# The x product of a tile ordered behind the next tile's gate and up gradients, and late gate-gradient tiles transposed by TensorE

## The chip, the cores and the metric

The kernel runs on one core of one Trainium2 chip. The metric is the device time of one execution in microseconds (us). The time before is the median of 8 runs, 528.19 us (527.13 to 531.25). The profile is of one execution, which itself took 527.57 us; its span, from the first to the last instruction of the program, is 525.8 us. The core's engines are called as the profile calls them: PE is TensorE (PEld its weight loads), DVE is VectorE, ACT is ScalarE, POOL is GpSimd and SP is SyncE, which here only issues DMAs.

## The reference

The program computes a forward block and its whole backward pass, for a sequence of 2048 rows of 512 columns in bf16:

```python
xn  = layernorm(x)                                   # x = A_q
s   = xn * (longconv(kv) + kv * ssm_D)               # kv = shiftconv(A_k) * A_v, the long convolution by FFT
z   = (sigmoid(xn @ w_gate) * (xn @ w_up)) @ w_down  # F = 1376
out = x + s * silu(z)
# outputs: out and the gradients of q, k, v, shift_k, ssm_k, ssm_D, w_gate, w_up, w_down for grad_out
```

What matters here is the backward pass of the gated unit. With h = sigmoid(g) * u, it needs for each block of 128 rows

- dz, the gradient of z: grad_out * s times the derivative of silu at z,
- dh = dz @ w_down^T, and from it dg and du, the gradients of the gate and up projections,
- dxn = dg @ w_gate^T + du @ w_up^T (the "x product"), plus what comes through s, and then the backward pass of the layernorm,
- later, over all rows, the three weight gradients.

## The kernel before, in words

**Tiling.** The 2048 rows are 16 tiles of 128 rows (NJ = 16), each [128, 512]; the 1376 columns of the hidden layer are padded to 11 blocks of 128 (NFB = 11), worked in three chunks of 4, 4 and 3 blocks (FBS).

**Stages.** In stage A (to about 155 us of the trace) the FFT convolution forward runs beside the forward products of nine of the tiles (FA, by `f_gen`). Stage B (`stepB`, line 1201, about 155 to 350 us) goes over the tiles i = 0 to 15 and does the remaining seven forward tiles and the backward pass of the gated unit. Stage C (about 350 us to the end) does the backward FFT convolution (`frontC`, `backC`) beside the weight gradients (`dW`), 35 blocks of 16 long matmuls each. `dW` already starts inside stage B, once tile 15's dz exists, and is what PE does alone in the last 16 us.

**The four steps of stage B**, each a Python generator which yields after a piece of work:

- `f_gen(i)` (719): 88 matmuls of 128 columns for gate and up, sigmoid, h; h goes to DRAM for the weight gradients.
- `z_gen(i)` (1114): 11 matmuls of 512 columns for z. Then a chain between ACT and DVE: sigmoid (1127), gate = z * sigmoid (1129), 1 - sigmoid (1131), three DVE steps to `dzA[:, i]` (1132 to 1134). dgate = grad_out * s (1121) enters in the last of these. Then the transpose `dzT`: for tiles 1 to 12 by a DMA transpose that SP issues (1137), for 0, 13, 14 and 15 by four PE transposes into PSUM and a copy (1139 to 1142). After that five more DVE steps (1144 to 1150): out, and `dxa`, the part of dxn that comes through s.
- `d_gen(i)` (1152): three chunks, 44 matmuls of 128 columns in all; each chunk is copied from PSUM by ACT and multiplied twice by DVE into `duT` and `dgT`, which SP also stores to DRAM. For the six tiles whose sigmoid and h were spilled in stage A (15, 13, 11, 9, 7, 5) DVE first forms v from them (two long steps, 1158 and 1159).
- `x_gen(i)` (1180): 22 matmuls of 512 columns into one PSUM bank, which read all of `duT` and `dgT`. Then on DVE dxn (1192, which reads PSUM and `dxa`), a product with a row sum (1193), a small step (1194), on ACT line 1195, on DVE 1196 and 1197; the result is written over the tile of grad_out (`goj`), and POOL stores it from there (1198).

**Order in the program.** Within turn i of the loop at 1209 the steps are: first part of d(i), a part of f(i+4), z(i+1), the loads of tile i+2 (`b_ld`, 1084, two DMAs on POOL), the rest of d(i) mixed with f(i+4), a reload of a spilled tile where there is one, the rest of f, and x(i).

**What the engines then do is set by a planner in the program.** All operations are recorded (`Rec.add`, 240) with a number n in program order and with what they depend on: overlapping SBUF bytes, DRAM blocks, PSUM tiles. `Rec.order` (348) then goes through a modelled time. Each engine takes the operation that can start earliest; of those ready when the engine comes free, the one with the smallest n. It looks ahead by 700 operations (LOOK), about four turns of the loop. It gives out the PSUM banks too: two each for long accumulations (psZ, psX and psW, kind "acc"), two for transposes ("tr"), four for single-bank products. So program order is a priority, and a step that isn't ready is passed over. The engines run their queues in the planned order, whatever comes late.

**Buffers** of stage B are rings (`Ring`, 93): a new use waits for the last reader of the slot. Those of interest: `dxa_r` 2 slots, `dxn_r` 2, `u1_r` 1, `dg_r` and `du_r` 2 each (1073 to 1080), the five tiles of the z chain (`zw`, 1060) one each, and `go_r`, the tiles of grad_out, 4 (1067, 1068). So grad_out of tile i+4 can be loaded once the store of x(i)'s result from the same slot has landed.

Of the kernel before, what the change touches and what calls it, by code (L numbers as in the profile page):

```python
# [20 lines left out]
D = 512  # L21
F = 1376
FP = 1408
NJ = 16
# [68 lines left out]
class Ring:  # L93
# [9 lines left out]
    def next(self):  # L103
        a = self.aps[self.i % len(self.aps)]
        self.i += 1
        return a
# [518 lines left out]
def kernel_impl(ctx, tc, A_q, A_k, A_v, A_shift_k, A_ssm_k, A_ssm_D, B_x, B_w_gate, B_w_up, B_w_down,  # L625
# [15 lines left out]
    ar = Arena(slab, SLAB)  # L641
# [4 lines left out]
    def ps_mm(shape, dt=f32, name=None):  # L646
        return nc.ps(PS["mm"], shape, dt)

    def ps_acc(shape, dt=f32, name=None):
        return nc.ps("acc", shape, dt)  # L650

    def ps_tr(shape, dt=bf16, name=None):
        return nc.ps("tr", shape, dt)
# [29 lines left out]
    def f_major(eng, dst, c, i, src):  # L683
        eng.dma_start(dst[c][i // 4, :, i % 4].rearrange("p (a t) -> p a t", t=128), src)
# [386 lines left out]
    wuT_r = Ring(ar, [NFB, D])  # L1071
    dz_r = Ring(ar, [NJ, D])
    dzA = dz_r.ap
    dxa_r = Ring(ar, [D], n=2)
    dzT_r = Ring(ar, [4, 128], n=2)
    dxn_r, u1_r = Ring(ar, [D], n=2), Ring(ar, [D])
    wq_r = Ring(ar, [NFB, 128])
    dh_r = Ring(ar, [4, 128], n=2)
    wd, wdT, wgT, wuT = wd_r.ap, wdT_r.ap, wgT_r.ap, wuT_r.ap
# [4 lines left out]
    def b_ld(i):  # L1084
        T[i]["x"], T[i]["go"] = xq2_r.next(), go_r.next()
        nc.gpsimd.dma_start(T[i]["x"], qC[:, i, :])
        nc.gpsimd.dma_start(T[i]["go"], goC[:, i, :])
# [17 lines left out]
    def w_gen():  # L1105
        pt = ps_tr([2, 4, 128], name="ps_w")
        for which, w in enumerate((wg, wu)):
            for db in range(4):
                nc.tensor.transpose(pt[:, which, db, :], w[:, db, FP - 128:FP], ident)
        for which, w in enumerate((wgT, wuT)):  # L1110
            nc.evac(w[:, NFB - 1, :].rearrange("p (c d) -> p c d", d=128), pt[:, which], 512)
        yield 1024

    def z_gen(i):
        hT, xj, goj = T[i]["h"], T[i]["x"], T[i]["go"]
        xn, y2 = xnA[:, i, :], y2A[:, i, :]
        psZ = ps_acc([D], name="psZ")
        s_out = zw["s_out"].next()
        dgate = zw["dgate"].next()
        nc.vector.tensor_tensor(s_out, xn, y2, ALU.mult)  # L1120
        nc.vector.tensor_tensor(dgate, goj, s_out, ALU.mult)
        for fb in range(NFB):
            nc.tensor.matmul(psZ[:], hT[:, fb, :], wd[:, fb, :], start=(fb == 0), stop=(fb == NFB - 1))
            if fb == 5:
                yield 6 * 512
        sigz = zw["sigz"].next()
        nc.scalar.activation(sigz, psZ[:], ACT.Sigmoid)
        gate = zw["gate"].next()
        nc.vector.tensor_tensor(gate, psZ[:], sigz, ALU.mult)
        t2 = zw["t2"].next()  # L1130
        nc.scalar.activation(t2, sigz, ACT.Identity, bias=1.0, scale=-1.0)
        nc.vector.tensor_tensor(t2, gate, t2, ALU.mult)
        nc.vector.tensor_tensor(t2, t2, sigz, ALU.add)
        nc.vector.tensor_tensor(dzA[:, i, :], dgate, t2, ALU.mult)
        T[i]["dzT"] = dzT_r.next()
        if 0 < i < NJ - 3:
            nc.sync.dma_start_transpose(T[i]["dzT"], dzA[:, i, :])
        else:
            pt = ps_tr([4, 128], name="ps_dzT")
            for db in range(4):  # L1140
                nc.tensor.transpose(pt[:, db, :], dzA[:, i, db * 128:(db + 1) * 128], ident)
            nc.evac(T[i]["dzT"], pt[:], 512)
        yield 5 * 512
        nc.vector.tensor_tensor(s_out, s_out, gate, ALU.mult)
        nc.vector.tensor_tensor(xj, xj, s_out, ALU.add)
        nc.gpsimd.dma_start(o0C[:, i, :], xj)
        nc.vector.tensor_tensor(gate, goj, gate, ALU.mult)
        T[i]["dxa"] = dxa_r.next()
        nc.vector.tensor_tensor(T[i]["dxa"], gate, y2, ALU.mult)
        nc.vector.tensor_tensor(y2, gate, xn, ALU.mult)  # L1150

    def d_gen(i):
        sigT, hT = T[i]["sig"], T[i]["h"]
        dzT = T[i]["dzT"]
        v = T[i].get("v")
        if v is None:
            v = wq_r.next()
            nc.vector.tensor_scalar(v, sigT, -1.0, 1.0, ALU.mult, ALU.add)
            nc.vector.tensor_tensor(v, v, hT, ALU.mult)
        yield 512  # L1160
        dgT, duT = dg_r.next(), du_r.next()
        T[i]["dg"], T[i]["du"] = dgT, duT
        for c, (f0, nb) in enumerate(FBS):
            psD = ps_mm([4, 128], name="psD")
            for b in range(nb):
                for db in range(4):
                    nc.tensor.matmul(psD[:, b, :], wdT[:, db, (f0 + b) * 128:(f0 + b + 1) * 128], dzT[:, db, :],
                                     start=(db == 0), stop=(db == 3))
            dh = dh_r.next()
            nc.scalar.copy(dh[:, 0:nb, :], psD[:, 0:nb, :])  # L1170
            nc.vector.tensor_tensor(duT[:, f0:f0 + nb, :], dh[:, 0:nb, :], sigT[:, f0:f0 + nb, :], ALU.mult)
            if T[i].get("v") is None:
                nc.vector.tensor_tensor(dgT[:, f0:f0 + nb, :], dh[:, 0:nb, :], v[:, f0:f0 + nb, :], ALU.mult)
            else:
                nc.vector.tensor_tensor(dgT[:, f0:f0 + nb, :], duT[:, f0:f0 + nb, :], v[:, f0:f0 + nb, :], ALU.mult)
            f_major(nc.sync, uF_d, c, i, duT[:, f0:f0 + nb])
            f_major(nc.sync, gF_d, c, i, dgT[:, f0:f0 + nb])
            yield nb * 512

    def x_gen(i):  # L1180
        dgT, duT, dxa, goj, xn = T[i]["dg"], T[i]["du"], T[i]["dxa"], T[i]["go"], xnA[:, i, :]
        psX = ps_acc([D], name="psX")
        n = 0
        for srcT, wT in ((duT, wuT), (dgT, wgT)):
            for fb in range(NFB):
                nc.tensor.matmul(psX[:], srcT[:, fb, :], wT[:, fb, :], start=(n == 0), stop=(n == 2 * NFB - 1))
                n += 1
                if n % 6 == 0:
                    yield 6 * 512
        dxn, u1, sm = dxn_r.next(), u1_r.next(), small.next()  # L1190
        r = rstd_all[:, i:i + 1]
        nc.vector.scalar_tensor_tensor(dxn, psX[:], 1.0, dxa, ALU.mult, ALU.add, accum_out=sm[:, 0:1])
        nc.vector.scalar_tensor_tensor(u1, dxn, 1.0, xn, ALU.mult, ALU.mult, accum_out=sm[:, 1:2])
        nc.vector.scalar_tensor_tensor(sm[:, 2:4], sm[:, 0:2], -1.0 / D, r.to_broadcast([P, 2]), ALU.mult, ALU.mult)
        nc.scalar.activation(u1, dxn, ACT.Identity, bias=sm[:, 2:3], scale=r)
        nc.vector.scalar_tensor_tensor(u1, xn, sm[:, 3:4], u1, ALU.mult, ALU.add)
        nc.vector.tensor_tensor(goj, u1, goj, ALU.add)
        nc.gpsimd.dma_start(o1C[:, i, :], goj)
        yield 4 * 512

    def stepB():
        f = f_gen(3)
        yield from w_gen()
        z = z_gen(0)
        for g in (f, z, f, z, f, z, f):
            c = next(g, None)
            if c:
                yield c
        for i in range(NJ):
            f = f_gen(i + LAG + 1) if i + LAG + 1 < NJ and i + LAG + 1 not in FA else iter(())  # L1210
            d, x = d_gen(i), x_gen(i)
            z = z_gen(i + 1) if i + 1 < NJ else iter(())

            def take(g, n):
                for _ in range(n):
                    c = next(g, None)
                    if c is None:
                        return
                    yield c
            yield from take(d, 1)  # L1220
            yield from take(f, 1)
            yield from take(z, 9)
            if i == NJ - 2:
                flags.add("z15")
            if i + 2 < NJ:
                b_ld(i + 2)
            for _ in range(3):
                yield from take(d, 1)
                yield from take(f, 1)
            yield from take(d, 9)  # L1230
            if i + LAG in FA[:NSP]:
                f_ld(i + LAG)
            yield from take(f, 9)
            yield from take(x, 9)
            if i + LAG + 1 == SEQ[-1]:
                flags.add("fwd")

    stC = {}
    jobs = [(s, c) for s in range(3) for c in range(3)]
# [167 lines left out]
    def gated(g, flag):  # L1407
        yield from g
        flags.add(flag)
    live = run_streams([(gated(stepB(), "B"), 447000, 0.0, 1.0)], until=lambda: "fwd" in flags)  # L1410
    for r in (wg_r, wu_r, xq_r, xnT_r):
        r.free()
# [108 lines left out]
```

## Time and profile before

| | before |
|---|---|
| median of 8 runs | 528.19 us (527.13 to 531.25) |
| the profiled execution | 527.57 us, span 525.8 us |
| PE, busy | 492.3 us (94%), 5373 matmuls |
| DVE, busy | 403.6 us (77%) |
| ACT, busy | 342.8 us (65%) |
| POOL, busy | 124.5 us (24%) |
| granted PE clock | 1.0 |
| chain that ended last | PE 48%, DVE 22%, ACT 10%, issue 8%, DMA 6% |

Busy is the time in which an engine executes something; the ends of matmuls are modelled, so PE's busy time holds some waiting. The chain that ended last is followed back from the last instruction, at each step to what released it. All instructions carry one source line, 512, that of the helper which emits the planned order, and nearly all SBUF operands are views of one tensor, `slab`. So groups are told apart by shape, and single steps by their place in the order: a weight load followed by a matmul of 512 columns is z, x or dW, one of 128 columns is d, f or a transpose; instruction k of an engine in the trace is operation k which the program emitted for it. Where a time of a single step of a named tile is given, it was found in that way.

### The profile page before, as it was taken

To read this page: it belongs to the slowest core of one execution; us is meant where nothing else is said; L and a number is where in the kernel's file an instruction comes from. 1 tells how busy PE (TensorE), PEld (TensorE's weight loads), DVE (VectorE), ACT (ScalarE), POOL (GpSimd) and SP (SyncE) were. 2 spreads that over 40 slices of the span, in tenths; PEclk is the share of its full clock that TensorE was granted. 3 is DMA by queue.
4 is the path that set the end of the run, shared out by engine and by line. 5 is a ranking of instruction groups with operands and counts; after the bars stand their busy time and mean duration, and the time that the engine had idled before them with its cause. 6 is when DMAs were issued, how large, how long until landed. Compare 5 with 4: busy or idle time off the path is not lost.

```text
span 525.8 us, 13494 instructions
## 1 busy us (share of the span) xinstructions
PE 492.3 (94%) x5373; PEld 350.4 (67%) x5429; DVE 403.6 (77%) x777; ACT 342.8 (65%) x455; POOL 124.5 (24%) x241
## 2 busy tenths in 40 slices
PE   4797898999999999999999999999899999999996
PEld 2786787888987676577775556554575665775744
DVE  7859989975759979978789999645758768883844
ACT  6899999999974345344443443335878968786621
POOL 5152523545613313424153221010000000000000
PEclk9999999999999999999999999999999999999999
DMA  8977798879999755647499946989699889999874
GB/s 259 260 223 273 226 337 200 264 221 272 252 184 218 159 162 144 206 124 184 121 226 262 202 130 196 232 289 241 131 234 245 208 242 245 265 192 252 196 216 118
DMA packets 173713, 113.19 MB, mean 215 GB/s; under 512 B 114487, under 2 KB 158161, under 8 KB 173394
## 3 DMA queue, kind: packets, MB, share of 16 engines
q1 hardware_dynamic: 162016, 78.43, 63.0%
q0 software_dynamic: 11104, 33.89, 20.9%
q8 instruction: 42, 0.69, 0.5%
q14 instruction: 21, 0.17, 0.1%
q10 hardware_dynamic: 530, 0.01, 0.1%
HBM read 37.65 MB, written 45.72 MB: 159 GB/s over the span
## 4 chain that ended last, share of the span: by engine, by line
PE 48%; DVE 22%; ACT 10%; issue 8%; DMA 6%; SPq 3%; POOL 2%; DVEq 0%; ACTq 0%; POOLq 0%
PE psum L512 48%; DVE slab L512 22%; ACT slab L512 10%; SPq L512 3%; DMA slab<-in_A_q_dram 1%; DMA slab<-in_B_w_up_dram 1%; DMA slab<-slab 1%; DMA slab<-in_A_k_dram 1%; DMA Ci_d<-slab 1%; DMA slab<-KK_d 1%; POOL slab L512 1%; POOL KK_d L512 0%; POOL hF_d L512 0%; POOL ksh_d L512 0%; POOL sF_d L512 0%
## 5 line engine op out<-in xcount | busy, mean ns | idle before, releaser
L512 PE MATMUL psum<-slab 128*128 128x128 bf16 (+4 forms) x5373 | 492.3, 253 | 29.4 <-ACT slab L512 13.0
L512 PEld LDWEIGHTS <-slab 128*128 128x128 bf16 (+2 forms) x5429 | 350.4, 99 | 170.9 <-issue 22.2
L512 DVE TENSOR_TENSOR slab<-slab 128x512 bf16<-128x512 bf16 (+6 forms) x472 | 268.6, 608 | 45.6 <-ACT slab L512 26.2
L512 ACT CAST slab<-psum 128x1024 bf16<-128x1024 f32 (+3 forms) x270 | 219.8, 860 | 96.5 <-PE psum L512 72.8
L512 ACT ACTIVATE slab<-psum 128x512 bf16<-128x512 f32 (+2 forms) x80 | 55.5, 694 | 46.0 <-PE psum L512 43.5
L512 ACT ACTIVATE slab<-slab 128x512 bf16<-128x512 bf16 (+2 forms) x53 | 42.1, 800 | 21.2 <-DVE slab L512 20.4
L512 ACT COPY slab<-psum 128x1024 bf16<-128x1024 bf16 (+1 forms) x49 | 46.7, 994 | 13.9 <-PE psum L512 13.9
L512 POOL DMA_DIRECT2D out_dram<-slab x32 | 17.5, 548 | 102.4 <-DVE slab L512 102.4
L512 DVE CAST slab<-psum 128x1024 bf16<-128x1024 f32 (+2 forms) x24 | 27.0, 1126 | 15.9 <-PE psum L512 14.8
L512 DVE TENSOR_TENSOR slab<-psum,slab 128x512 bf16<-128x512 f32 (+2 forms) x47 | 29.3, 626 | 12.3 <-ACT slab L512 7.6
L512 DVE SCALAR_TENSOR_TENSOR slab<-slab 128x512 bf16<-128x512 bf16 (+2 forms) x64 | 28.0, 438 | 7.9 <-POOL slab L512 5.7
L512 POOL DMA_DIRECT2D hF_d<-slab x48 | 26.1, 547 | 32.6 <-DVE slab L512 32.4
L512 POOL MEMSET slab<- 128x128 bf16 (+3 forms) x11 | 4.3, 401 | 118.2 <-PE psum L512 117.8
L512 DVE SCALAR_TENSOR_TENSOR slab<-psum,slab 128x512 bf16<-128x512 f32 x16 | 11.0, 688 | 21.3 <-PE psum L512 21.2
L512 POOL DMA_DIRECT2D KK_d<-slab x32 | 17.5, 548 | 21.7 <-ACT slab L512 18.5
L512 POOL DMA_DIRECT2D slab<-in_A_q_dram x29 | 16.2, 558 | 22.8 <-ACT slab L512 18.7
L512 DVE TENSOR_SCALAR slab<-slab 128x1 f32<-128x1 f32 (+9 forms) x54 | 16.4, 324 | 2.2 <-ACT slab L512 1.2
L512 DVE STREAM_TRANSPOSE slab<-slab 128x1024 f32<-128x1024 f32 x8 | 14.3, 1823 | 4.3 <-ACT slab L512 4.3
L512 POOL DMA_DIRECT2D slab<-hF_d x18 | 9.7, 543 | 10.6 <-PE psum L512 9.8
L512 POOL TENSOR_TENSOR slab<-slab 128x1 f32<-128x1 f32 x16 | 9.8, 613 | 9.5 <-DVE slab L512 9.3
L512 DVE BATCH_NORM_STATS2 slab<-slab 128x6 f32<-128x512 bf16 x16 | 11.0, 686 | 1.4 <-DMA slab<-in_A_q_dram 1.4
L512 POOL DMA_DIRECT2D slab<-in_grad_out_dram x16 | 8.7, 541 | 6.4 <-DMA out_dram<-slab 5.0
(20 smaller groups left out, 32.7 us busy)
## 6 DMA issues: line engine op xcount, KB each, us to landing
KK_d<-slab POOLq DMA_DIRECT2D x32, 256.0 KB, 4.7
slab<-KK_d SPq DMA_DIRECT2D x16, 512.0 KB, 4.5
slab<-in_A_v_dram SPq DMA_DIRECT2D x4, 1024.0 KB, 9.3
hF_d<-slab POOLq DMA_DIRECT2D x32, 128.0 KB, 4.3
slab<-slab SPq DMA_DIRECT2D x32, 128.0 KB, 4.8
out_dram<-slab POOLq DMA_DIRECT2D x32, 128.0 KB, 3.2
uF_d<-slab SPq DMA_DIRECT2D x32, 128.0 KB, 2.4
gF_d<-slab SPq DMA_DIRECT2D x32, 128.0 KB, 2.2
```

What stands on the lines that cost most here:

```text
L512: getattr(getattr(self.nc, eng), meth)(*[place(v) for v in a], **{x: place(v) for x, v in k.items()})
```

## The change

Three things are edited.

1. In the loop of `stepB`, turn i now carries x(i-1) in the place of x(i); turn 0 has no x, and x(15) follows behind the loop. In program order x(i-1) then stands behind d(i) and z(i+1).
2. `dxa_r` gets a third slot, as `dxa` of a tile now lives a turn longer, and `dxn_r` loses its second. Each slot has 1024 bytes per partition, so the total is as before; `dzT_r`, which lies between them, moves by 1024 bytes.
3. The DMA transpose of dz is used for tiles 1 to 9, where it was 1 to 12. Tiles 10, 11 and 12 now take the PE path.

```diff
-    dxa_r = Ring(ar, [D], n=2)
+    dxa_r = Ring(ar, [D], n=3)
     dzT_r = Ring(ar, [4, 128], n=2)
-    dxn_r, u1_r = Ring(ar, [D], n=2), Ring(ar, [D])
+    dxn_r, u1_r = Ring(ar, [D]), Ring(ar, [D])
@@ z_gen
-        if 0 < i < NJ - 3:
+        if 0 < i < 10:
             nc.sync.dma_start_transpose(T[i]["dzT"], dzA[:, i, :])
         else:
             pt = ps_tr([4, 128], name="ps_dzT")
             for db in range(4):
                 nc.tensor.transpose(pt[:, db, :], dzA[:, i, db * 128:(db + 1) * 128], ident)
             nc.evac(T[i]["dzT"], pt[:], 512)
@@ stepB
-            d, x = d_gen(i), x_gen(i)
+            d, x = d_gen(i), x_gen(i - 1) if i else iter(())
             z = z_gen(i + 1) if i + 1 < NJ else iter(())
...
             yield from take(x, 9)
             if i + LAG + 1 == SEQ[-1]:
                 flags.add("fwd")
+        yield from x_gen(NJ - 1)
```

## The prediction

> **What bounds the kernel now.** I read the page first, then busy time by stretch, then the chain and the waits of the stretch that stood out. The columns of the busy time are the length, then PE, weight loads, DVE, ACT and POOL, each with its number of instructions, PE's clock and DMA:
>
> ```profile
> PE 492.3 (94%) x5373; PEld 350.4 (67%) x5429; DVE 403.6 (77%) x777; ACT 342.8 (65%) x455; POOL 124.5 (24%) x241
> ```
> ```profile
> 200.00:240.00 40.00, 39.44 (x418) 27.47 (x420) 35.87 (x93) 18.99 (x34) 13.50 (x25) 1.00 0.52 150
> 240.00:277.00 37.00, 36.90 (x386) 25.53 (x386) 29.57 (x72) 15.95 (x29) 14.52 (x27) 1.00 0.75 193
> 277.00:324.00 47.00, 44.55 (x366) 26.55 (x368) 45.16 (x116) 18.49 (x33) 13.05 (x26) 1.00 0.73 188
> 324.00:350.00 26.00, 25.79 (x178) 14.27 (x181) 15.27 (x41) 7.54 (x14) 2.03 (x4) 1.00 0.94 234
> ```
>
> Stage B has two regimes. To 277 us the forward tiles fill PE and DVE has slack: 4.1 us idle in the first stretch shown, 7.4 in the second. At 277 the last forward tile is done. To 324 DVE is busy 96% and PE idles; from 324 the weight gradients fill PE again. The chain of the middle stretch says the same:
>
> ```profile
> by line: DVE slab L512 58.6%; PE psum L512 30.1%; issue 11.1%; DVEq L512 0.3%
> ...
> 312.97 0.20 issue
> 313.17 0.76 DVE slab L512 x2
> 313.98 6.07 PE psum L512 x54
> ```
>
> From 277.0 to 314.0 it runs on DVE with hardly a gap, then on PE. PE's weight loads there show where it paid:
>
> ```profile
> 280.67 1.41 PEld L512 LDWEIGHTS <-slab 128*128 128x128 bf16 x8 [0.29 <-DVE slab L512]
> 283.33 8.62 PEld L512 LDWEIGHTS <-slab 128*128 128x128 bf16 x75 [1.26 <-DVE slab L512]
> 292.30 0.55 PEld L512 LDWEIGHTS <-slab 128*128 128x128 bf16 x4 [0.35 <-DVE slab L512]
> 293.03 8.10 PEld L512 LDWEIGHTS <-slab 128*128 128x128 bf16 x72 [0.18 <-DVE slab L512]
> 302.38 0.64 PEld L512 LDWEIGHTS <-slab 128*128 128x128 bf16 x5 [1.25 <-issue]
> ```
>
> Four of these stand inside an x product that waits for the last `duT` or `dgT` which DVE has yet to multiply. Taking the distance of successive weight loads less their regular distance (55 ns before a matmul of 128 columns, 216 ns before one of 512), PE's real stalls in stage B are: 0.50 us at 167.3 (x(0) waits for the transposed up weights), 0.72 at 218.1 (x(4)), 1.47 at 280 to 282 (x(9)), 0.23 at 291.9 (x(10)), 1.24 at 301.0 (a piece of stage C taken in as filler waits for ACT), 0.20 at 303.1 (x(11)) and 0.71 at 313.1 (x(12)). The sum is 5.1 us, of which 1.2 fall in the first regime and 3.85 in the second. That is the most an order of stage B can give back. It would reach the end in full: PE has weight gradients waiting until the last instruction, and nothing else ends late.
>
> **What the Trainium skill says.** "Perfetto Trace Analysis", Optimization Strategy: the most contended engine can change over a kernel, and mixing the regimes can then help. The trace agrees: PE, then DVE from 277 us, then PE. "TensorE: Matmul & The Clock Gate", Part 4: a PE transpose of 128x128 takes about 275 ns in a kernel and its PSUM result must be copied out. Here the four transposes of tile 13 start 55 ns apart; the trace's number is used. The copy is there (ACT, 587 ns). "DMA: Bandwidth & Descriptors", Anatomy of one DMA: each DMA has a fixed 2 us or so, most of it the receipt at the end. The trace's own loads and stores on POOL take 2.2 to 5.9 us to land, so a ring slot which has to be stored and reloaded costs two of these.
>
> **The change part by part.** The numbers of matmuls, multiplications and stores stay; DVE's work stays exactly.
>
> *Transposes.* Removed: three DMA transposes, each 1.2 us of SP's queue and 4.6 to 5.1 us to landing (tiles 10 to 12: issued 278.8, 286.7, 298.2, landed 283.6, 291.8, 302.8). Added: 12 PE transposes of 55 ns, 0.66 us of PE, and three ACT copies of 0.59 us on an engine that is busy 18.5 of 47 us. From the last dz step to `dzT` it took 5.2 to 7.0 us for tiles 10 to 12; for 13 and 14, on PE, 1.3 and 1.5 us. So d can start some 4 to 5 us earlier. Stores of dg and du, which queue behind these transposes on SP, come earlier too. Of the 0.66 us I count 0.3, since PE has 3.85 us of holes there; without the holes it is 0.66.
>
> *The order.* x(i-1) now stands behind d(i), so its `duT` and `dgT` were multiplied a step before. Stalls of x on DVE (0.72 + 1.47 + 0.23 + 0.20 + 0.71 = 3.33 us) have no cause left where this order is what the planner emits. In its place PE needs d(i+1) sooner. From z(i+1)'s last matmul to its dz it is 5.0 to 6.7 us for tiles 11 to 15 (279.4 to 284.8, 290.9 to 297.6, 300.9 to 307.2, 312.3 to 317.4, 322.6 to 327.6). A PE transpose takes `dzT` to 6.6 to 7.6 us behind z. x(i-1) covers 4.75 of that (22 x 216 ns). The remaining 2 to 3 us are covered by a forward tile to 277 and after that by x(i), which the planner may take early. At the start, x(0) moves behind z(2) and perhaps d(1), and its 0.50 us wait for the weights goes.
>
> *DVE.* In rows of the DVE-bound stretch, a tile costs: x, 0.685 + 0.719 + 0.16 + 0.719 + 0.421 and two accumulator reads of 0.082, 2.87 us; z, 0.684 + 10 x 0.421, 4.89; d, 4 x 0.421 + 2 x 0.353, 2.39, and 0.519 + 0.888 more for a spilled tile. On PE they cost 4.75, 2.37 and 2.77. Preferring d and z to x exchanges 4.75 us of PE work with 2.87 of DVE for 5.14 with 7.28. So at 277 us DVE could be up to 4.4 us further, out of the 7.4 it idles before. At the end an x is left over to the time after 324, where DVE has 10.7 us to spare. This is what can lift the bound of the middle stretch. I take half of its 3.85 us, as the loads of grad_out (below) keep z from running far ahead; the ends are 0 and 3.85.
>
> *Buffers.* One `dxn` slot: it is free again after the ACT step, some 3 us after the x product, and the next comes at least 4.75 us later; cost nothing, and about 1 us once for x(14) and x(15) if that cover goes.
>
> *The sum*, against the profiled execution: -1.2 (first regime) -1.9 (second) +0.3 (transposes) +0.5 for new waits of d on `dzT` to 277, where the DMA transposes land 2.4 to 5.1 us after issue (ends 0 and 2) = -2.3 us. Span 525.8 to 523.5, execution 527.57 to 525.3. The median stands 0.6 us above the profiled execution: **525.9 us**. Stage C keeps its operations and program order but is planned anew from another start; its waits I put at 1 us either way.
>
> **Rivals.** *The grad_out ring becomes the wait (slower).* POOL's queue shows the load of a grad_out tile straight behind the landing of an x result:
>
> ```profile
> 303.46 0.55 POOL L512 DMA_DIRECT2D out_dram<-slab  x1 [4.25 <-DVE slab L512]
> 304.00 0.54 POOL L512 DMA_DIRECT2D slab<-in_A_q_dram  x1
> 308.28 0.54 POOL L512 DMA_DIRECT2D out_dram<-slab  x1 [3.74 <-DVE slab L512]
> 308.82 0.54 POOL L512 DMA_DIRECT2D slab<-in_grad_out_dram  x1
> ```
>
> x(10) ends on PE at 295.9, its result is stored at 303.5 and has landed at 305.9, grad_out of tile 14 is loaded at 308.8 and lands at 311.3, 15.4 us in all; dgate(14) needs it at 315.0. From landing to the gate step of the same tile there are 4.8, 8.4, 3.2, 4.0 and 3.9 us for tiles 11 to 15. If x(i) moves back by a d and a z (5.14 us) and z keeps its place, dgate comes late by 0.3, 0, 1.9, 1.1 and 1.2 us, 4.5 in all, on DVE, which is the bound there and runs in order. Behind it on DVE stand the multiplications of d, and for those PE waits. With 0.66 for the transposes and 1.2 gained earlier: +4, 532. It decides once x(i) falls back against z(i+4) by more than 3.2 us. Against it: the planner knows this dependence, and can hold to x(i) earlier.
>
> *DVE stays the bound (same).* Its work in the middle stretch is unchanged, so the 3.85 us only move; -1.2 + 0.66 gives 527.6. For it: DVE's chain without gaps. Against it: idle DVE before 277.
>
> *The order hardly changes (same).* The planner passes over what isn't ready; if d(i+1) never is when x(i-1) could go, x comes where it came. For it: it already runs d(8) and z(10) around x(8). Then only the transposes remain, 528.3.
>
> **How the numbers follow.** Faster as worked out 0.40, the ring 0.36 (with any other new wait on the way from z to d in its neighbourhood), DVE stays 0.14, order unchanged 0.10. About 0.3%, 1.6 us, is what a measurement of this kernel can tell from no change: faster 0.40, same 0.24, slower 0.36. The first case by itself reaches from 523.4 (all 5.1 us back, 0.3 paid, stage C as before) to 526.6. Leaving out some 0.08 below (stage C gains too) and 0.12 above (ring waits in each of five tiles with z further ahead, or stage C over 1 us worse), the range is 523.2 to 532.5.
>
> **What would show it.** Right: in the middle stretch PE's waits for DVE inside x products gone, DVE busier than 29.6 of 37 us before 277, the last forward tile ending at about the same time, PE filled again by weight gradients before 324. Ring: POOL's grad_out loads landing later than the gate steps, DVE waiting for DMA. DVE stays: DVE still over 95% busy over some 45 us. Unchanged order: d, z, x in the old succession. What makes it wrong altogether: a stage C whose waits moved by more than 2 us.

## The result and the profile after

The changed kernel takes 535.25 us (median of 22 executions, 532.73 to 539.24) beside 529.55 us for the kernel before on the same chip (59 executions). The ratio is 1.0109, 95% interval 1.0090 to 1.0129: 1.1% slower, where 525.9 us and faster was forecast. Ratios here and below compare the executions within 1.5% of the fastest of their kernel; slower ones, 10 of 18 and 8 of 13 in two of the versions below, are left out. The profiled execution took 535.66 us, 8.1 more than that of before; its span is 533.9 us.

Engine totals of the kernel after, from its page:

```profile
PE 494.4 (93%) x5380; PEld 351.3 (66%) x5441; DVE 407.4 (76%) x779; ACT 343.1 (64%) x456; POOL 125.0 (23%) x241
```

The work is the same to 1%. The time lies between: the first d product starts at 161.7 us (160.8 before), the last x product ends at 355.8 (349.7), and the last instruction of an engine ends at 530.7 (522.5). So 0.9 us are lost in stage A, which the change does not touch (there PE's clock was at half for 3.4 us from 24.8 us on, and in the profile of before it was not), 5.2 in stage B and 2.1 in stage C. Busy time by stretch, in the columns of the prediction (length, then PE, weight loads, DVE, ACT, POOL, PE's clock, DMA):

```profile
200.00:240.00 40.00, 37.91 (x409) 27.04 (x413) 33.87 (x86) 17.34 (x32) 13.07 (x23) 1.00 0.49 144
240.00:277.00 37.00, 36.59 (x334) 23.35 (x337) 33.61 (x82) 14.52 (x26) 15.08 (x28) 1.00 0.73 200
277.00:324.00 47.00, 44.47 (x408) 28.28 (x412) 40.32 (x101) 19.02 (x34) 12.27 (x25) 1.00 0.66 170
324.00:350.00 26.00, 24.72 (x180) 13.86 (x182) 18.09 (x49) 7.24 (x13) 2.03 (x4) 1.00 0.95 228
```

DVE is further at 277 us, as forecast: 33.61 us of work in the second stretch, where it was 29.57. But in the middle stretch it is busy 40.32 of 47 us where it was 45.16, and PE gains nothing (44.47 for 44.55). The chain that ended last, in that stretch of the kernel after:

```profile
by line: DVE slab L512 63.5%; PE psum L512 16.7%; issue 9.5%; ACT slab L512 7.0%; DMA out_dram<-slab 3.9%; DVEq L512 0.4%
...
305.31 0.71 DVE slab L512 x2
306.24 0.82 ACT slab L512
307.08 0.76 DVE slab L512
307.87 1.37 DVE slab L512 x3
309.34 0.44 DVE slab L512
```

The chain of before in the same stretch (the one shown ahead of the result runs to 330 us):

```profile
by line: DVE slab L512 66.1%; PE psum L512 21.5%; issue 12.4%; DVEq L512 0.3%
```

The path still runs on DVE, and PE's share fell from 21.5% to 16.7%. New is the ACT piece: line 1195 of an x step, for which DVE stands still in the middle of its own chain (1194 before it, 1196 behind it). Waits of the kernel after from 160 to 345 us (engine, line and what it waited for; total, times, longest, in us), DVE's first, then PE's, then ACT's:

```profile
DVE slab L512 <- ACT slab L512: 11.6, 13, 1.4
DVE slab L512 <- PE psum L512: 2.6, 2, 1.4
```
```profile
PE psum L512 <- DVE slab L512: 3.6, 7, 0.9
PE psum L512 <- ACT slab L512: 1.8, 2, 1.3
PE psum L512 <- DMA slab<-slab: 1.5, 1, 1.5
```
```profile
ACT slab L512 <- DVE slab L512: 77.8, 29, 6.7
```

The kernel before, DVE and then ACT:

```profile
DVE slab L512 <- PE psum L512: 15.5, 6, 4.5
DVE slab L512 <- ACT slab L512: 0.2, 1, 0.2
```
```profile
ACT slab L512 <- DVE slab L512: 25.2, 21, 3.3
```

Before, DVE waited for PE, which is slack, and hardly for ACT. After, it waits 13 times for ACT, and ACT 29 times for DVE. ACT's queue runs in order, and x's step stands in it ahead of the sigmoid of the next z: for z(4), (5) and (7) the sigmoid starts 2.2, 3.6 and 2.8 us after z's last matmul (0.5, 0.5 and 0.6 before). The weight loads show where PE pays (column in brackets: idle before, and what ended it):

```profile
273.46 11.14 PEld L512 LDWEIGHTS <-slab 128*128 128x128 bf16 x125 [0.69 <-DVE slab L512]
285.23 13.06 PEld L512 LDWEIGHTS <-slab 128*128 128x128 bf16 x125 [0.62 <-DVE slab L512]
298.97 10.56 PEld L512 LDWEIGHTS <-slab 128*128 128x128 bf16 x86 [0.69 <-DVE slab L512]
310.73 9.05 PEld L512 LDWEIGHTS <-slab 128*128 128x128 bf16 x79 [1.20 <-DVE slab L512]
321.19 9.05 PEld L512 LDWEIGHTS <-slab 128*128 128x128 bf16 x79 [1.41 <-DVE slab L512]
```

These are no longer x products that wait for `duT` or `dgT`. Each is a PE transpose of dz, queued inside an x product, whose dz DVE has not made yet: tiles 10 to 14. By the prediction's measure (distance of weight loads less the regular distance) they cost 0.57, 0.67, 0.57, 1.08 and 1.29 us; with tile 15's (1.02), the piece of `dW` beside it (0.64), d(1) waiting for its DMA transpose at 169.3 (1.89), and f(8) and f(10) waiting for ACT at 210.3 and 235.9 (1.48, 0.68), and a small one, the stalls of stage B are 10.1 us. They were 5.1.

**The planner saw none of this.** In its own time the plan of the changed kernel ends 0.36 us earlier than that of before (508.10 for 508.46). From the first d to the end of the last x it plans 185.3 us; the trace has 194.0, 8.7 more. For the kernel before it is 186.1 planned, 188.9 in the trace, 2.8 more. What it misjudges can be read from one group of the kernel before, in the middle stretch:

```profile
L512 DVE TENSOR_TENSOR slab<-slab 128x512 bf16<-128x512 bf16 x73 | 28.2, 421 | 1.3
```

The planner reckons 0.068 us and 512 elements at 1920 per us (lines 314 to 321), 335 ns. The trace has 421. The Trainium skill ("VectorE: DVE Perf Modes", The TRN2 errata — SBUF-src ops pay a fixed extra latency per instruction) says that its table's fixed 58 cycles (60 ns, close to the planner's 68) under-predict a single operation, and that 150 cycles of 0.96 GHz are measured. With the planner's two elements per cycle (1920 per us) that makes an estimate of (150 + 256) / 0.96 = 423 ns, and the 421 ns of this trace agree. But how long a step takes is not how soon the next can start. Of neighbouring pairs of such steps in stage B of the kernel before, the 95 in which the second does not need the first start 0.33 to 0.34 us apart, which is the planner's figure; 80 of the 81 in which it does start 0.45 to 0.46 us apart. So the planner is right for free steps and 0.12 us short for each step of a chain, and z and x hold such chains.

### The profile page after: what moved, and what is told of

It is laid out like the page before. It is cut to its first block, busy times and chain, and to the rows that moved or that the text cites. A ratio compares the mean times of both kernels' runs of the same rounds, so it can differ in the third digit from the quotient of the medians.

```text
span 533.9 us, 13509 instructions
## 1 busy us (share of the span) xinstructions
PE 494.4 (93%) x5380; PEld 351.3 (66%) x5441; DVE 407.4 (76%) x779; ACT 343.1 (64%) x456; POOL 125.0 (23%) x241
## 4 chain that ended last, share of the span: by engine, by line
PE 37%; DVE 28%; ACT 17%; issue 9%; DMA 6%; POOL 1%; SPq 0%; another core or an unknown queue 0%; DVEq 0%; ACTq 0%; POOLq 0%
PE psum L512 37%; DVE slab L512 28%; ACT slab L512 17%; DMA out_dram<-slab 1%; DMA slab<-in_A_q_dram 1%; DMA uF_d<-slab 1%; DMA slab<-slab 1%; DMA slab<-KK_d 1%; DMA sF_d<-slab 1%; POOL KK_d L512 0%; POOL slab L512 0%; SPq L512 0%; POOL hF_d L512 0%; DVEq L512 0%
## 5 line engine op out<-in xcount | busy, mean ns | idle before, releaser
L512 PE MATMUL psum<-slab 128*128 128x128 bf16 (+5 forms) x5380 | 494.4, 253 | 35.4 <-ACT slab L512 15.4
L512 PEld LDWEIGHTS <-slab 128*128 128x128 bf16 (+2 forms) x5441 | 351.3, 99 | 178.1 <-issue 24.8
L512 ACT CAST slab<-psum 128x1024 bf16<-128x1024 f32 (+4 forms) x268 | 218.0, 860 | 98.5 <-PE psum L512 60.1
L512 ACT COPY slab<-psum 128x1024 bf16<-128x1024 bf16 (+1 forms) x52 | 48.5, 969 | 13.3 <-PE psum L512 13.3
L512 DVE CAST slab<-psum 128x1024 bf16<-128x1024 f32 (+2 forms) x26 | 28.9, 1113 | 16.1 <-PE psum L512 13.8
L512 DVE STREAM_TRANSPOSE slab<-slab 128x1024 f32<-128x1024 f32 x8 | 14.3, 1830 | 4.6 <-ACT slab L512 4.6
```

The source lines that it names most:

```text
L512: getattr(getattr(self.nc, eng), meth)(*[place(v) for v in a], **{x: place(v) for x, v in k.items()})
```

## The experiments

The theory of the prediction was gone with the result: x's waits for DVE are removed as forecast, and others twice as large have come. First the change was taken apart, then the buffer, then the single waits, and last the planner's price. PE stalls are those of stage B, by the same measure, in the profiled execution of each.

### The parts

Transposes alone (the kernel before):

```diff
-        if 0 < i < NJ - 3:
+        if 0 < i < 10:
```

> The kernel before with tiles 10 to 12 of dz transposed by PE; order and rings as before. Theory T: 1.003 to 1.006 (12 PE transposes, 0.66 us, and waits of 0.5 us or more at each of the three). Theory O: z's chain is not behind an x tail here, so the transposes find dz in time: 0.998 to 1.002, and no wait over 0.3 us at them.

Rings alone (the kernel before):

```diff
-    dxa_r = Ring(ar, [D], n=2)
+    dxa_r = Ring(ar, [D], n=3)
-    dxn_r, u1_r = Ring(ar, [D], n=2), Ring(ar, [D])
+    dxn_r, u1_r = Ring(ar, [D]), Ring(ar, [D])
```

> The kernel before with three dxa slots and one dxn slot; order and transposes as before. Theories T, O and G: nothing of the loss, 0.997 to 1.003. If the single dxn slot or the moved addresses made the loss, 1.006 or more.

Order and rings, without the new PE transposes (the kernel after):

```diff
-        if 0 < i < 10:
+        if 0 < i < NJ - 3:
```

> The changed kernel with tiles 10 to 12 of dz transposed by DMA as before; only the order of x and the rings are changed. Theory T (PE transposes): the trace of the changed kernel shows PE waiting 1.8 us at the transposes of tiles 10 to 12, inside x products, and each costs 0.22 us; if these made the loss, this runs at 1.000 to 1.003 of before. Theory O (order): x's DVE and ACT tail now stands in front of the next z chain, which makes dz late whoever transposes it; then this runs at 1.006 to 1.012, and waits of d on the DMA transposes replace those at the PE transposes. Theory G (grad_out ring): 1.008 or more, with POOL waits for landings of x results as in the changed kernel.

And with all transposes but tile 0's by DMA (the kernel after):

```diff
-        if 0 < i < 10:
+        if 0 < i:
```

> The changed kernel with all of tiles 1 to 15 of dz transposed by DMA, so that no PE transpose stands inside an x product. The changed kernel's waits at its six PE transposes sum to 5.2 us. Theory T: they go, 0.999 to 1.002 of before. Theory O: dz is still late, PE then waits for d or runs other work; 1.006 or more.

| | ratio to before | 95% interval | PE stalls, us |
|---|---|---|---|
| the whole change | 1.0109 | 1.0090 to 1.0129 | 10.1 |
| transposes alone | 1.0001 | 0.9975 to 1.0026 | 4.4 |
| rings alone | 1.0111 | 1.0070 to 1.0152 | 9.6 |
| order and rings | 1.0123 | 1.0087 to 1.0158 | 10.6 |
| order and rings, all by DMA | 1.0112 | 1.0068 to 1.0156 | 14.3 |

The transposes are worth nothing either way, and the edit that looked like bookkeeping, the rings, costs all of the 1.1% by itself. It is the third `dxa` slot: with `dxn` on one slot and `dxa` still on two, the planned order of PE, DVE, ACT and POOL is that of the kernel before, operation for operation. The chain of rings alone, from 277 to 324 us:

```profile
by line: DVE slab L512 85.9%; issue 14.3%; DVEq L512 0.5%
```

PE does not appear in it at all. Here the x products still wait for `duT` and `dgT`, more than before: x(10) 0.99 us, x(11) 1.26 in two pieces, x(12) 0.80, x(13) 1.26; PE transposes of dz(13) and dz(14), queued between them, wait 0.73 and 0.41 us. So the third slot costs the same in two programs of different order, through different waits. The 14.3 us of the last row are from an execution of 542.2 us (median 539.4) and hold two waits for DMA transposes, of 4.4 and 6.2 us.

### The slot

What the slot gives the planner is a freedom. With two slots, `dxa` of tile i+2 (lines 1149 and 1150, z's last two steps) can't be written before dxn(i) (1192) has read its own. To take the freedom back with the new slots in place, the dependence is written down: rings alone, with

```diff
-        nc.vector.tensor_tensor(T[i]["dxa"], gate, y2, ALU.mult)
+        o = nc.vector.tensor_tensor(T[i]["dxa"], gate, y2, ALU.mult)
+        if i > 1:
+            o.deps.add(T[i - 2]["dxn"])
```

> The kernel before with the changed rings (three dxa slots, one dxn slot), and the planner told that dxa of tile i may not be written before dxn of tile i-2, as two slots enforce. The planned order of every engine is then that of the kernel before; only addresses differ. Theory S (the third slot costs through the order in which DVE's steps are then planned): 0.997 to 1.003 of before. If one dxn slot or the addresses cost: 1.007 or more, as with the rings alone.

Measured 0.9999 (0.9971 to 1.0027), stalls 4.6 us: neither the address nor the single `dxn` slot costs anything. The same dependence in the whole change, where it is added when x(i) is recorded, for tile i+2:

```diff
-        nc.vector.scalar_tensor_tensor(dxn, psX[:], 1.0, dxa, ALU.mult, ALU.add, accum_out=sm[:, 0:1])
+        o = nc.vector.scalar_tensor_tensor(dxn, psX[:], 1.0, dxa, ALU.mult, ALU.add, accum_out=sm[:, 0:1])
+        if i + 2 < NJ:
+            T[i + 2]["o"].deps.add(o.n)
```

> The changed kernel, in which the planner may write dxa of tile i+2 only after x(i) has read its own, as two slots enforced it: the new program order and the PE transposes remain, the third slot's freedom goes. If the freedom of the slot is the whole cause: 0.997 to 1.004. If the new program order itself costs: 1.008 to 1.013. In the planned order four of sixteen tiles have nothing between dxn and the step after ACT, against nine of the changed kernel, so I expect 1.003 to 1.007, some 3 us less than the changed kernel.

1.0003 (0.9976 to 1.0031). The new program order and the PE transposes are still there, and the loss is gone. (Its profiled execution, 534.6 us, lies 3.3 above its median and is not read.) I had expected 1.003 to 1.007, because four tiles in that plan leave DVE nothing to do during ACT's step; those holes turn out cheaper than I took them for. Holding z's last five steps instead of two:

```diff
-        nc.vector.tensor_tensor(s_out, s_out, gate, ALU.mult)
+        T[i]["o"] = nc.vector.tensor_tensor(s_out, s_out, gate, ALU.mult)
```

> The changed kernel with the five last DVE steps of z(i+2) held by the planner until dxn of tile i has been computed. In the plan one to three of them then stand between x's small step (1194) and the step that needs ACT's result (1196), for all tiles but the last; in the changed kernel there are none for nine of the tiles, and DVE stands still for 0.88 us each time. Theory W (DVE, the bound, waits for ACT inside each x): DVE's waits for ACT in stage B fall from 11.6 us to under 4, and the time to 1.003 to 1.007 of before. Theory D (what is left is transfers that collide in the changed order and z's chain behind x's): 1.008 or more in spite of it.

1.0087 (1.0048 to 1.0126): a longer hold is not a better one. Why is not shown: it also delays steps on which stores and ring slots depend, but its profiled execution (548.0 us) was the longest of its fifteen. DVE's waits for ACT in it are 7.8 us, not under 4 as expected. To see whether any other order costs 1%, the kernel before was planned with a slightly shorter look ahead:

```diff
-LOOK = 700
+LOOK = 690
```

> The kernel before with the planner's look-ahead at 690 operations in place of 700: the same work, order and rings, planned anew from 77 us on. It asks what a new plan costs by itself. If the loss is the rule for any new plan: 1.006 or more. If the third slot, the order and the transposes each have a cause of their own: 0.997 to 1.003.

1.0002 (0.9970 to 1.0034), stalls 4.6. This tells less than it was meant to: the plan differs from 77 us on, but from 160 to 350 us every engine's order is that of the kernel before, operation for operation. That another order of stage B need not be slow is shown further down, by the kernel before with the planner's higher price (1.0004).

### The single waits

x's ACT step on DVE (the kernel after), so that DVE and ACT no longer wait for each other there:

```diff
-        nc.scalar.activation(u1, dxn, ACT.Identity, bias=sm[:, 2:3], scale=r)
+        nc.vector.tensor_scalar(u1, dxn, r, sm[:, 2:3], ALU.mult, ALU.add)
```

> The changed kernel with x's one ACT step (line 1195) done by DVE (same arithmetic, some 0.3 us more of DVE a tile), so that no ACT step of x stands in ACT's queue ahead of the next sigmoid. In the changed kernel ACT waits 78 us for DVE in stage B, before 25. Theory A (ACT's queue): sigmoids start within 0.7 us of z's last matmul, dz comes 1 to 2 us earlier, 1.002 to 1.006. If ACT's queue is no cause: 1.010 to 1.013.

1.0079 (1.0051 to 1.0107). DVE's waits for ACT fell from 11.6 to 2.4 us, PE's stalls only from 10.1 to 9.6. The interval overlaps that of the whole change, so no more than some 0.3% is shown for this wait, the one that stands out most in the profile. DVE has sixteen more steps here, and PE's clock was at half for 3.4 us in the profile, so the wait and its remedy are not cleanly parted.

The planner told that dz is ready for PE's transposes 1.5 us later than it thinks (the kernel after), so that they are queued later (`lag`, new, is added to the time at which an operation becomes ready):

```diff
-                nc.tensor.transpose(pt[:, db, :], dzA[:, i, db * 128:(db + 1) * 128], ident)
+                nc.tensor.transpose(pt[:, db, :], dzA[:, i, db * 128:(db + 1) * 128], ident).lag = 1.5
```

> The changed kernel, whose planner takes dz to be ready for PE 1.5 us later than it computes, so that the PE transposes stand that much later in PE's queue. Theory P: the 5.2 us of waits at the six transposes mostly go, 1.001 to 1.005 of before. Theory S and the order by itself: DVE is late by the same amount, and the wait turns up at d's matmuls or in x's products: 1.008 or more.

1.0106 (1.0074 to 1.0139): the waits moved, and the loss stayed (PE's order changes little: 35 of its 1722 operations of stage B stand elsewhere). DVE now waited 5.5 us for the reload of tile 13's spilled sigmoid, which took 15.8 us to land among many other transfers.

The rival of the prediction, the grad_out ring, had its own test. x's result is written over `dxa` and stored from there, so that the grad_out slot is free one store earlier (the kernel after):

```diff
-        nc.vector.tensor_tensor(goj, u1, goj, ALU.add)
-        nc.gpsimd.dma_start(o1C[:, i, :], goj)
+        nc.vector.tensor_tensor(dxa, u1, goj, ALU.add)
+        nc.gpsimd.dma_start(o1C[:, i, :], dxa)
```

> The changed kernel, with the x result written over dxa and stored from there, so that a grad_out slot is free again as soon as x(i) has read it, one store of some 2 us earlier, and the dxa slot is held longer instead. If the grad_out ring is what became the wait (the rival of the prediction): 1.000 to 1.006. If not: 1.008 to 1.014. I expect the latter.

1.0103 (1.0073 to 1.0133). No gain. In the profile of after, grad_out of tiles 11 to 15 lands 2.0, 1.3, 1.6, 4.5 and 4.6 us ahead of the step that reads it (1121). POOL's queue, by the side of the lines shown for before:

```profile
311.77 0.55 POOL L512 DMA_DIRECT2D out_dram<-slab  x1 [2.63 <-DVE slab L512]
312.31 0.54 POOL L512 DMA_DIRECT2D slab<-in_grad_out_dram  x1
319.25 0.54 POOL L512 DMA_DIRECT2D out_dram<-slab  x1 [6.39 <-DVE slab L512]
322.23 0.54 POOL L512 DMA_DIRECT2D out_dram<-slab  x1 [2.44 <-DVE slab L512]
322.76 0.54 POOL L512 DMA_DIRECT2D slab<-in_grad_out_dram  x1
```

The load still follows right behind the landing of an x result, and POOL waits for DVE, not the other way round.

Two side tests. z's last five steps put behind x(i-1) in the program, `dxa` and `dxn` on two slots each (the kernel after; its last steps of tile 15 read tiles already given away, so it does not compute what it should, and its time is only indicative):

```diff
-            yield from take(z, 9)
+            yield from take(z, 2)
...
             yield from take(x, 9)
             if i + LAG + 1 == SEQ[-1]:
                 flags.add("fwd")
+            yield from take(z, 9)
```

> The changed order and PE transposes, but the last five DVE steps of z(i+1) (out, dxa, the gradient of s) stand behind x(i-1) in program order, so that two dxa slots and two dxn slots are enough, as before. Theory S (third slot): with three slots these steps run on DVE ahead of x's and d's steps, which the ring of two had held back; held back again, this comes to 0.998 to 1.004 of before. Theory P (PE transposes in a queue that waits for dz): the tail stands behind dz anyway, so dz comes no earlier: 1.007 or more.

1.0061 (1.0029 to 1.0094), between the two ranges expected, so it decides nothing. And 1 - sigmoid of d (1158) on ACT in the kernel before, to see what less work on DVE is worth. The step is made for nine tiles, 0, 1 and 2 beside the six with a spilled sigmoid; in the trace of before, those of 11 and 13 fall at 293.3 and 304.6 us:

```diff
-            nc.vector.tensor_scalar(v, sigT, -1.0, 1.0, ALU.mult, ALU.add)
+            nc.scalar.activation(v, sigT, ACT.Identity, bias=1.0, scale=-1.0)
```

> The kernel before with the step 1 - sigmoid of the six spilled tiles (line 1158, 0.52 us on DVE) done by ACT. If DVE bounds 277 to 324 us in the kernel before, taking 0.52 us from it for each of tiles 9 to 15 with odd numbers gives 1 to 2 us: 0.996 to 0.998. If PE or the chains between engines bound it: 0.999 to 1.002.

0.9993 (0.9970 to 1.0016): no gain is shown. But a gain of up to 1.6 us is not excluded, and only two of the nine steps, 1.0 us, come off DVE from 277 to 324 us, so this does not decide whether DVE's work bounds that stretch.

### The planner's price

If the cause is that the planner spends the slot's freedom on the strength of DVE steps that are too short, a higher price must take the loss away, with the slot, the order and the transposes in place. In `Rec.order`:

```diff
                 occ, lat = self.cost(alt)
+                if e == "vector" and 150 < t < 345 and self.size(alt[2][0]) > 100:
+                    occ, lat = occ + 0.09, lat + 0.09
```

The kernel after with it:

> The changed kernel, whose planner reckons 0.09 us more for each large DVE step in stage B. A step of 128x512 then stands in its books at 0.42 us, which is what it takes in the traces, and not at 0.33. Theory W in its general form (the changed order is planned with DVE's steps too short, so that DVE's idle time looks free): 1.000 to 1.005, with two or three steps between 1194 and 1196 again. If the order is bad whatever the planner knows: 1.008 or more.

Rings alone with it:

> The two rings of the change alone (three slots for dxa, one for dxn) cost 1.1% with the planner as it is, and without that DVE waited for ACT. Here the planner reckons a large DVE step of stage B 0.09 us longer and nothing else differs. Theory (the loss is the order that a planner with too short DVE steps picks once the slot is free): back to 0.997 to 1.003, PE stalls in stage B from 9.6 us to about 5. Rival (the third slot itself costs, by its place in memory or by what it lets run ahead): 1.008 to 1.014, PE stalls stay at 9 us or more.

And the kernel before with it:

> The kernel before with the same 0.09 us in the planner. Theory (two slots already forced a good order, so the right price adds little): 0.996 to 1.002. Rival (the right price by itself is worth 1%, and the changed kernel with it is then still 1% behind what the old rings would give): 0.985 to 0.993.

The 0.09 us go on every large DVE step alike. They bring the commonest one to 0.42 us, its duration, which lies between the two distances above; and x's three long steps, planned at 0.74 us for 0.69 to 0.75 in the trace of before, are overpriced with them. So this is a higher price rather than an exact one.

| | as it was | with the price | 95% interval | PE stalls, us | stage B planned, in the trace |
|---|---|---|---|---|---|
| the whole change | 1.0109 | 0.9983 | 0.9955 to 1.0012 | 10.1, now 2.7 | 188.5, 188.6 |
| rings alone | 1.0111 | 0.9988 | 0.9953 to 1.0023 | 9.6, now 1.2 | 188.9, 186.8 |
| before | 1 | 1.0004 | 0.9970 to 1.0038 | 5.1, now 7.0 | 188.9, 191.8 |

Of the 7.0 us in the last row 3.4 are one wait, d(1) for its DMA transpose.

Both losses are gone. The planned length of stage B fits the trace of the whole change to 0.1 us, where it was 8.7 short; for the other two it is 2.1 us too long and 2.9 too short, so the fit to 0.1 says little by itself. The chain from 277 to 324 us, first of the whole change with the price, then of rings alone with it:

```profile
by line: PE psum L514 86.4%; DVE slab L514 7.6%; ACT slab L514 4.9%; issue 1.3%
...
276.91 20.16 PE psum L514 x185
```
```profile
by line: PE psum L514 87.0%; DMA slab<-slab 8.9%; ACT slab L514 3.2%; issue 1.1%
```

In both, the chain of the middle stretch is PE's, which neither kernel had reached. That alone is no measure of the time: it is PE's for 83.5% in the kernel before with the price, which is no faster than before, and for 60.3% in order and rings, which has the whole loss. Waits of the whole change with the price, 160 to 345 us, DVE's and then ACT's:

```profile
DVE slab L514 <- ACT slab L514: 12.3, 24, 1.5
DVE slab L514 <- PE psum L514: 1.6, 1, 1.6
```
```profile
ACT slab L514 <- DVE slab L514: 7.9, 5, 3.4
```

DVE waits for ACT as long as in the slow kernel (12.3 us for 11.6), so that this total, the most striking line of the profile after, is no measure of the loss. ACT's wait for DVE did go, 77.8 us before the price and 7.9 with it. But it is no measure of the loss either: in rings alone, with the same loss, it is 30.6 us, for 25.2 in the kernel before, and DVE waits only 1.1 us for ACT. The number of DVE steps queued between 1194 and 1196, tiles 0 to 15, shows the order:

```
before             3 3 2 3 3 3 2 3 2 4 4 3 3 3 2 0
rings alone        3 3 2 3 4 0 3 3 2 3 4 4 2 2 2 0
rings, with price  2 3 3 2 2 2 2 3 2 2 4 2 2 2 3 0
after              2 2 0 0 1 0 1 0 0 0 0 0 1 0 1 1
after, with price  2 3 2 2 3 2 3 2 2 2 3 2 2 2 0 0
```

In the kernel before the two slots hold z's last two steps back, and in seven of the sixteen tiles these fill the gap in x. With the slot free the planner runs them ahead: in rings alone it queues `dxa` of tile i+2 in front of dxn(i) for six of fourteen tiles, in the whole change for all fourteen. But it does not take them back with the higher price: there it is five and fourteen. What fills x's gap in the whole change with the price is the first steps of a later z and the two long steps of a d (1158, 1159). And in rings alone the gap is hardly emptier than before, with d's multiplications in the place of z's steps.

So two things are shown, each in two programs: the loss goes when the slot's freedom is taken back, and it goes with the freedom in use when the planner's DVE steps cost more. What is not shown is which displaced step costs the time: the price moves 336 of PE's 1722 operations of stage B in the whole change, and 530 of 1707 in rings alone, so that much else changes with it.

None of these versions is clearly faster than the kernel before.

## Why the prediction was wrong

- **"Stalls of x on DVE have no cause left"**: right as far as it went. No x product of the changed kernel waits for `duT` or `dgT`. But the step that counted them as gain (-1.2 and -1.9) failed: PE met the same late DVE one step earlier, at the transposes of dz, and the stalls doubled. I costed the wait that goes and bounded the new wait on `dzT` at 0 to 2 us by the landing of DMA transposes alone; the transposes on PE, where x stands behind them in PE's queue, were not in that bound.
- **"DVE could be up to 4.4 us further at 277 us"**: measured 3.7 (105.3 us of work from 160 to 277 for 101.6). But being further did not lift the bound: part of it was work that nothing needed yet, z's last steps, and at the next dz DVE was late all the same. Whether DVE's work is the bound there stays open: 1158 off DVE (0.9993, 0.9970 to 1.0016) does not decide it.
- **Buffers**: "one `dxn` slot, cost nothing" is right (0.9999 with the old order held). What I did not ask is what the slot that was *added* sets free. That is the term that was missing from the sum, and it is 1.1% by itself. I took the third slot to belong to the order and priced it at nothing.
- **The planner**: I treated it as something that knows the dependences. I had its cost formula and the 421 ns row in front of me, used the row, and did not compare the two. 2.8 us of stage B's length stood unplanned already before; in the changed order it became 8.7.
- **Transposes, +0.3**: alone 1.0001 (0.9975 to 1.0026), 0 with an uncertainty of 1.3 us. That agrees, and is too coarse to tell 0.3 from 0 or from the full 0.66.
- **"It would reach the end in full"**: wrong. With the price, rings alone has 1.2 us of PE stalls for 5.1, and its time is that of before. In its profile stage B is 2.1 us shorter, and the last step of ACT ends at 520.9 us, where it was 522.2. But "nothing else ends late" fails: the last three stores, which SP issues one behind the other, start with DVE's last step, which ends at the same time as before. SP, first in rings alone with the price, then in the kernel before:

```profile
518.75 3.87 SPq L514 DMA_DIRECT2D out_dram<-slab  x3
518.68 3.87 SPq L512 DMA_DIRECT2D out_dram<-slab  x3
```

So in this profile PE's gain ends in front of SP. Whether that is the rule was not followed up.

- **Stage C, 1 us either way**: 2.1 us longer in this profile. 0.4 us of it, by the matmuls counted in both traces, is PE work that before had already done when the last x ended; the rest is open.
- **The rivals**: the size of the first (532 us) is nearest, but the ring is not its cause, as its own test showed. "Any other new wait on the way from z to d in its neighbourhood", which I had put with it, is what came in the profile. The "order hardly changes" rival failed most plainly: with the rings alone, where the program's order does not change at all, the planned order changed enough for the whole loss. (Its 528.3 us is not the sum of its parts either: 528.19 with 0.3 to 0.66 for the transposes is 528.5 to 528.9.)

What stays open is how the 1.1% splits over the single waits: no wait taken alone gave back more than some 0.3%. That the planner's DVE prices decide what it makes of the slot rests on two kernels out of two. An order that uses the slot, is planned with the old prices and is unlike these two was not tried, nor was a wrong price of another size: the versions with dz later and with all transposes by DMA, which stayed at 1.0106 and 1.0112, are close copies of the changed kernel's plan (2 and 5 of 366 DVE steps of stage B stand elsewhere).

## What to carry to other kernels

Before adding a buffer to a kernel that a planner orders, ask what the old number of buffers forced, since a shortage can be holding a good order in place; and compare the planner's price of the commonest instruction with the profile, its duration and the distance from start to start, with and without a dependence, before trusting the order it makes of the new freedom. A wait that a reordering removes is a gain only if the producer is not late for the next consumer as well. The largest new wait in a profile need not be the loss: a version without the loss can show the same total, and one with the loss can lack it.

## What was unexpected of the hardware

**The granted clock.** In order and rings, d(12) waited 4.1 us for its DMA transpose at 303.7 us, which stood on SP behind two others:

```profile
292.09 12.27 SPq L512 DMA_TRANSPOSE slab<-hF_d  x2
304.46 1.21 SPq L512 DMA_TRANSPOSE slab<-slab  x1
```

After it PE ran at half its clock for 3.4 us, in busy time by stretch of the same kernel:

```profile
303.00:308.00 5.00, 1.27 (x6) 0.39 (x5) 3.80 (x9) 1.92 (x3) 1.62 (x3) 1.00 1.20 215
308.40:311.80 3.40, 3.40 (x31) 2.92 (x28) 3.23 (x9) 1.12 (x2) 0.54 (x1) 0.51 0.60 191
```

With all transposes by DMA it came twice, after stalls of 4.4 us (3.4 us at half clock) and 6.2 us (6.8). The Trainium skill ("TensorE: Matmul & The Clock Gate", Part 1) puts the halving behind at least one idle window of about 3.4 us. The half-clock stretches of these traces agree with such a window: each lasts 3.41 us or two or three times that. The waits agree only in part. All eight waits of over 3.7 us in stage B of the profiles of this study met the half clock. Shorter ones went both ways: a wait of 3.4 us in the kernel before with the price left the clock whole, and with x's ACT step on DVE the half clock followed a wait of PE for ACT of 2.1 us by the weight loads, 1.9 by PE's busy time (212.2 to 214.2):

```profile
211.00:214.20 3.20, 1.26 (x24) 1.14 (x22) 2.04 (x6) 2.46 (x5) 0.59 (x1) 1.00 0.36 127
215.32:218.73 3.41, 3.41 (x24) 2.31 (x22) 3.24 (x9) 1.59 (x4) 1.08 (x2) 0.50 0.46 108
```

So these traces show no length below which a wait is safe. A stall that meets it costs more than itself: 1.7 us of work for 3.4 us at half the clock. Stage B of the kernel before has no half-clock stretch; its longest stall is 1.2 us.

**Single transfers.** In some variants of the changed order, h's transposes, a tile's stores and two tiles' loads fall together at 290 to 305 us. With dz taken later, a load of 128 KB took 15.6 us to land there and the reload of a spilled sigmoid (352 KB) 15.8; in stage B of the kernel before no load or store took over 6.3 us, in the changed kernel itself none over 7.1.
